# Attention, SwiGLU and eight routed experts on one core: where the overflow branch stands against the last expert's two scatters

## The chip, the core and the metric

The kernel runs on one core of a Trainium2 chip. The metric is device time in microseconds (us), the median of several runs. Inside the core five engines run their own instruction streams: TensorE (PE, with its weight loads as PEld), VectorE (DVE), ScalarE (ACT), GpSimd (POOL) and SyncE (SP). They meet only through semaphores. Each has a sequencer that runs waits, branches, register loads and DMA issues; in the trace those rows carry a q behind the engine's name (POOLq, SPq).

## The reference, cut to what matters

Three stages follow each other on 1536 tokens of width 512: an attention with local and global keys, a SwiGLU layer after an RMS norm, and a mixture of eight experts of which each token takes one. Only the last is touched:

```
logits = x @ w_gate
expert_idx = np.argmax(logits, axis=1)
...
for e in range(E):
    mask = expert_idx == e
    xe = x[mask]
    h = np.maximum(xe @ w1[e], 0.0)
    ye = h @ w2[e]
    out[mask] = gate_w[mask, None] * ye
```

The expert's width is 1024. Every row of `out` is written by exactly one expert.

## The kernel before, in words

**Two program paths.** Two input numbers, n_global and n_local, decide at run time whether a fast attention may be used. The whole of the rest, `body(is_fast)`, is built twice, and a branch of all five engines chooses (line 1339, `tc.If(fast == 1)` with `cmp.Else()`). The first copy, the fast one, runs here; the second copy's instructions lie behind it in each engine's program and are jumped over at the end.

**The experts.** Each expert has 256 slots (CAP), kept as two lists of 128 token numbers and gate weights. For each expert the kernel gathers its tokens' rows from DRAM, multiplies them with w1 (line 1044), takes the positive part on ACT and DVE (lines 1052 and 1053), multiplies with w2 (line 1022) and writes the result back. `expert_pair` does this for a whole expert, and ends in `second_layer`, which for each half of 128 tokens runs 24 matmuls into one PSUM bank `py`, scales the bank by the gate weight on ACT into a tile `yo` (line 1028), and has POOL issue an indirect DMA, the scatter, which writes the 128 rows of `yo` to the places in `out` that the token list names (line 1029):

```
1028  nc.scalar.activation(out=yo, in_=py, func=ACTF.Copy, scale=gwl[j])
1029  nc.gpsimd.indirect_dma_start(
1030      out=out, out_offset=bass.IndirectOffsetOnAxis(ap=idxl[j], axis=0),
1031      in_=yo, in_offset=None, bounds_check=NT - 1, oob_is_err=False,
```

Expert 0 goes another way in its first 128 tokens (`expert_tile`), experts 1 to 7 go through `expert_pair`. All weights of the last expert are loaded and converted long before its matmuls end.

**Tokens over capacity.** After the last expert comes `overflow` (line 1096). It counts the tokens of each expert with one small matmul, makes `need`, a row of flags, on DVE, and then every engine loads the first flag into a register (line 1111) and branches on it (line 1112, `tc.If(any_ == 1)`). With these inputs no expert has more than 256 tokens, so the branch's body is not run. The part that stands for the body not run (called the untaken side here) is not empty: on every engine it waits until the engine's own work is done and steps its semaphores by what the body would have added. For POOL this is a row of waits for the eight semaphores of its indirect DMAs, the last two scatters' among them, and then an instruction INC_SWDGE_SEM that adds to the eight. Then a branch leads to the end of the program (line 1380).

**The end.** At line 1380 SP waits for every semaphore of the program (12 rows of waits), all engines drain, POOL waits for the other four, clears the semaphores and releases them.

**What sets the order.** The order on each engine is made by a scheduler, which keeps to the program's order of the stages; the counting and the flags were already put early (near 460 us). PE, DVE, ACT and SP reach the branch as their own last instruction allows; POOL reaches it when it has issued the last scatter.

Of the kernel before, what the change touches and what calls it, by code (L numbers as in the profile page):

```python
# [8 lines left out]
F32 = mybir.dt.float32  # L9
F32R = mybir.dt.float32r  # L10
BF16 = mybir.dt.bfloat16
U32 = mybir.dt.uint32
I32 = mybir.dt.int32
ACTF = mybir.ActivationFunctionType
ALU = mybir.AluOpType
# [4 lines left out]
P = 128  # L20
B, H, S, D = 2, 8, 768, 64
NT, DM, DFF = B * S, H * D, 1536
NE, DF2 = 8, 1024
KD = DM // P
NP = H // 2
TT = NT // P
# [13 lines left out]
CAP = 256  # L40
FULL = NT
# [4 lines left out]
def kernel(  # L46
# [16 lines left out]
    nc = tc.nc  # L63
# [103 lines left out]
    rp = ctx.enter_context(tc.tile_pool(name="rp", bufs=1))  # L167
# [116 lines left out]
    for x in (tab0, tabL, tabG):  # L284
        half = const.tile([P, x.shape[1]], F32, name="half" + str(len(tabs)))
        nc.scalar.activation(out=half, in_=x, func=ACTF.Copy, scale=0.5)
        tabs.append((x, half))

    warm(WARM0)
    fast = nc.values_load(flag, min_val=0, max_val=1)  # L290

    def body(is_fast):
# [17 lines left out]
        def ps_mm(name):  # L310
            tag = banks["mm"][banks["n"] % len(banks["mm"])]
            banks["n"] += 1
            return ps(tag, {"mm": NMM, "s": NS, "pt": NPT}[tag], name)
# [698 lines left out]

        last_mm = {}

        def second_layer(hid, w2t, idxl, gwl, between):

            for j in range(len(idxl)):
                py = ps_mm("py")
                n = 0
                for m in range(DF2 // P):  # L1020
                    for a, c in ((0, 0), (0, 1), (1, 0)):
                        last_mm["py"] = nc.tensor.matmul(  # L1022
                            out=py, lhsT=hid(m, a, j), rhs=w2t[m // 2][:, c, (m % 2) * DM:(m % 2 + 1) * DM],
                            start=(n == 0), stop=(n == 23),
                        )
                        n += 1
                yo = rp.tile([P, DM], F32, tag="cv", bufs=2, name="yo")
                nc.scalar.activation(out=yo, in_=py, func=ACTF.Copy, scale=gwl[j])  # L1028
                nc.gpsimd.indirect_dma_start(  # L1029
                    out=out, out_offset=bass.IndirectOffsetOnAxis(ap=idxl[j], axis=0),  # L1030
                    in_=yo, in_offset=None, bounds_check=NT - 1, oob_is_err=False,
                )
                between()

        def expert_pair(w1t, w2t, idxl, gwl, xs, between):

            xsh, xsl = xs
            ht = []
            for m in range(DF2 // P):
                ph = ps_mm("ph")  # L1040
                n = 0
                for kk in range(KD):
                    for a, x in ((0, xsh), (0, xsl), (1, xsh)):
                        nc.tensor.matmul(  # L1044
                            out=ph[:, 0:CAP], lhsT=w1t[kk][:, a, m * P:(m + 1) * P], rhs=x[:, kk, :],
                            start=(n == 0), stop=(n == 3 * KD - 1),
                        )
                        n += 1
                if m % 2 == 0:
                    ht.append(hid_tile("eh"))  # L1050
                hi, lo = (ht[-1][:, a, (m % 2) * CAP:(m % 2 + 1) * CAP] for a in range(2))
                nc.scalar.activation(out=hi, in_=ph[:, 0:CAP], func=ACTF.Relu)  # L1052
                nc.vector.scalar_tensor_tensor(  # L1053
                    out=lo, in0=ph[:, 0:CAP], scalar=0.0, in1=hi.bitcast(F32), op0=ALU.max, op1=ALU.subtract
                )
                between()
            second_layer(
                lambda m, a, j: ht[m // 2][:, a, (m % 2) * CAP + j * P:(m % 2) * CAP + (j + 1) * P],
                w2t, idxl, gwl, between,
            )  # L1060

        def expert_tile(w1t, w2t, idx, gw, xs, between, high_first=False):
# [30 lines left out]
            )  # L1093


        def overflow(eb):
            XC = (FULL - CAP) // CAP
            cn = ps("x", 1, "cn")
            nc.tensor.matmul(out=cn[:, 0:NE], lhsT=ones, rhs=ohsum, start=True, stop=True)
            cnt = eb.tile([P, NE], F32, name="cnt")  # L1100
# [5 lines left out]
            for c in range(XC):  # L1106
                nc.vector.tensor_scalar(
                    out=need[:, 1:].rearrange("p (e c) -> p c e", c=XC)[:, c, :], in0=cnt[0:1, :],
                    scalar1=float(CAP * (c + 1)), scalar2=None, op0=ALU.is_gt,
                )  # L1110
            any_ = nc.values_load(need[:, 0:1], min_val=0, max_val=1)  # L1111
            with tc.If(any_ == 1):
                SLOTS = FULL - CAP
# [184 lines left out]
        def idx(e):  # L1298
            return [tks[:, 2 * e + j - 1:2 * e + j] for j in range(2)]

        def gw(e):
            return [wts[:, 2 * e + j - 1:2 * e + j] for j in range(2)]
# [4 lines left out]
        for e in range(NE):  # L1307
# [17 lines left out]
            if e == 0:  # L1325
                x = expert_tile(w1t.pop(0), w2t.pop(0), tks[:, 0:1], wts[:, 0:1], xs.pop(0), between)
                for _ in range(KD):
                    next(x)
                turn_rows(xg.pop(1), x=x1, js=(1,), after=last_mm["ph"])
                xs[1] = x1[:, 0], x1[:, 1]  # L1330
                drain(x)
            else:
                expert_pair(w1t.pop(e), w2t.pop(e), idx(e), gw(e), xs.pop(e), between)
        overflow(rp)
        ea_cm.__exit__(None, None, None)
        bctx2.close()

# [2 lines left out]
        body(True)  # L1340
    with cmp.Else():
        body(False)


def bits(x):
# [39 lines left out]
```

## Time and profile before

| what | value |
|---|---|
| median of 3 runs | 655.94 us (652.44 to 659.27) |
| the profiled execution | 662.28 us |
| its span (first to last instruction) | 660.2 us |
| time around the span | 2.08 us |
| PE busy | 637.3 us (97% of the span) |
| DVE, ACT, POOL busy | 445.2, 318.2, 187.3 us |
| mean granted clock of PE | 0.957 |

The profile is that of one execution, with times from the span's start. "Idle before" is what an engine waited ahead of an instruction, and the arrow names what ended that wait. Busy time leaves out sequencer rows (waits, branches, register loads), though they take time on their engine; they are found by the line that they belong to.

### The profile page before, as it was taken

How to read it: one execution, taken by the hardware profiler on the slowest of the kernel's cores; microseconds unless marked ns; L12 is line 12 of the kernel's file. 1: busy time of each engine (PE TensorE's matmuls, PEld its weight loads, DVE VectorE, ACT ScalarE, POOL GpSimd, SP SyncE). 2: the span in 40 equal slices, each digit the busy share in tenths (PEclk: the TensorE clock that was granted, in tenths of full speed). 3: DMA queues.
4: the chain of work that ended last, by engine and by line, in shares of the span. 5: the costliest groups of instructions: out<-in, count | busy, mean ns of one | idle time of the engine just before them, and what ended most of it. 6: DMA issues, size and time to landing. Idle time of an engine off the chain costs nothing. (4 is left out here: it accounts for less than half of the span.)

```text
span 660.2 us, 11655 instructions
## 1 busy us (share of the span) xinstructions
PE 637.3 (97%) x4280; PEld 570.1 (86%) x4281; DVE 445.2 (67%) x1090; ACT 318.2 (48%) x624; POOL 187.3 (28%) x259
## 2 busy tenths in 40 slices
PE   8999989999999999999999999999999999999991
PEld 3577989999999999999999999997888898899891
DVE  3845699987389998676349998953667565664410
ACT  2745678788465553334622211343656464554410
POOL 4432265354121232121122523471611121011000
PEclk9955789999999999999999999999999999999997
DMA  7644456742015443221311020342877668454001
GB/s 226 159 144 111 116 166 179 201 122 60 7 36 157 131 157 97 65 97 65 128 64 38 28 65 33 99 144 96 288 265 257 209 205 266 156 190 141 17 12 31
DMA packets 56567, 82.98 MB, mean 126 GB/s; under 512 B 7983, under 2 KB 38703, under 8 KB 56496
## 3 DMA queue, kind: packets, MB, share of 16 engines
q1 hardware_dynamic: 53552, 74.75, 37.0%
q0 software_dynamic: 2944, 7.35, 3.3%
q8 instruction: 37, 0.61, 0.4%
q14 instruction: 34, 0.28, 0.1%
HBM read 75.75 MB, written 7.39 MB: 126 GB/s over the span
## 5 line engine op out<-in xcount | busy, mean ns | idle before, releaser
L774 PE MATMUL pg<-xn,gv 128*128 128x256 f32 x1728 | 225.1, 283 | 0.2 <-DVE hf L787 0.2
L774 PEld LDWEIGHTS pg<-xn,gv 128*128 128x128 f32 x1728 | 217.1, 190 | 6.3 <-DVE hf L787 0.7
L811 PE MATMUL po<-ow,hid 128*128 128x512 f32 x432 | 113.8, 396 | 1.1 <-POOL hid L792 1.0
L792 POOL TENSOR_TENSOR hid<-hf,hid 128x256 fp32r<-128x256 f32 x72 | 63.5, 884 | 163.3 <-ACT hid L791 163.2
L1022 PE MATMUL py<-ew,eh 128*128 128x512 f32 x384 | 91.2, 395 | 1.2 <-ACT eh L1088 0.8
L811 PEld LDWEIGHTS po<-ow,hid 128*128 128x128 f32 x432 | 75.9, 188 | 13.7 <-POOL hid L792 1.5
L1022 PEld LDWEIGHTS py<-ew,eh 128*128 128x128 f32 x384 | 71.3, 188 | 18.0 <-ACT eh L1088 1.0
L1044 PE MATMUL ph<-xs,ew 128*128 128x256 f32 x672 | 83.1, 283 | 0.0
L1044 PEld LDWEIGHTS ph<-xs,ew 128*128 128x128 f32 x672 | 81.6, 191 | 0.7
L791 ACT ACTIVATE hid<-hf 128x256 fp32r<-128x256 f32 x72 | 29.8, 416 | 80.7 <-DVE hf L787 79.2
L1029 POOL DMA_INDIRECT out_dram<-yo,tk x16 | 16.5, 1034 | 138.5 <-ACT yo L1028 106.9
L843 DVE CUSTOM_DVE_ANT_0 jk<-duo,rgb 128x512 bf16<-128x512 f32 x64 | 54.3, 848 | 0.5
L962 DVE TENSOR_TENSOR ew<-rawe,ew 128x1024 fp32r<-128x1024 f32 (+1 forms) x36 | 40.8, 1134 | 13.0 <-ACT ew L958 10.9
L567 ACT ACTIVATE pr<-pr,mx 128x256 f32<-128x256 f32 (+1 forms) x96 | 42.3, 483 | 14.3 <-DVE mx L563 14.3
L1053 DVE SCALAR_TENSOR_TENSOR eh<-ph,eh 128x256 fp32r<-128x256 f32 x56 | 23.2, 422 | 37.9 <-ACT eh L1052 36.7
L782 ACT ACTIVATE th<-pg 128x256 f32<-128x256 f32 x72 | 27.1, 379 | 41.0 <-PE pg L774 40.6
L962 DVE TENSOR_TENSOR ew<-duo,ew 128x1024 fp32r<-128x1024 f32 x28 | 34.1, 1224 | 18.0 <-ACT ew L958 17.0
L958 ACT ACTIVATE ew<-rawe 128x1024 fp32r<-128x1024 f32 x36 | 38.1, 1059 | 10.7 <-PE pg L774 4.7
L1052 ACT ACTIVATE eh<-ph 128x256 fp32r<-128x256 f32 x56 | 21.1, 384 | 39.3 <-PE ph L1044 38.3
L783 DVE SCALAR_TENSOR_TENSOR th<-th,pg 128x256 f32<-128x256 f32 x72 | 29.7, 414 | 14.5 <-ACT th L782 13.5
L958 ACT ACTIVATE ew<-duo 128x1024 fp32r<-128x1024 f32 x28 | 29.4, 1059 | 19.4 <-PE py L1022 19.4
L820 DVE TENSOR_TENSOR duo<-duo,po 128x512 f32<-128x512 f32 x36 | 23.3, 682 | 22.2 <-PE po L811 22.1
(179 smaller groups left out, 930.3 us busy)
## 6 DMA issues: line engine op xcount, KB each, us to landing
rawe<-in_moe_w_dram SPq DMA_DIRECT2D x36, 512.0 KB, 4.9
duo<-in_moe_w_dram SPq DMA_DIRECT2D x28, 512.0 KB, 5.6
raw<-in_moe_w_gate_dram SPq DMA_DIRECT2D x12, 512.0 KB, 4.1
raw<-in_moe_w_val_dram SPq DMA_DIRECT2D x12, 512.0 KB, 6.0
raw<-in_moe_w_out_dram SPq DMA_DIRECT2D x12, 512.0 KB, 3.5
kn<-in_k_dram SPq DMA_DIRECT2D x28, 192.0 KB, 3.2
qn<-in_q_dram SPq DMA_DIRECT2D x36, 128.0 KB, 3.2
vn<-in_v_dram SPq DMA_DIRECT2D x16, 192.0 KB, 2.6
```

The costliest lines, as they stand in the source:

```text
L567: pin["act"] = nc.scalar.activation(out=pr[:, j, 0:n], in_=pr[:, j, 0:n], func=ACTF.Exp, bias=mx[:, t, j:j + 1], scale=-1.0,)
L774: nc.tensor.matmul(out=pg[:, 0:n_], lhsT=gv[:, i, a, kk, :], rhs=x[st][:, kk, :], start=(n == 0), stop=(n == 3 * KD - 1),)
L782: pin["th"] = nc.scalar.activation(out=th, in_=pss[0][:, 0:n_], func=ACTF.Tanh, scale=0.5)
L783: nc.vector.scalar_tensor_tensor(out=th, in0=th, scalar=1.0, in1=pss[0][:, 0:n_], op0=ALU.add, op1=ALU.mult)
L791: nc.scalar.activation(out=hh[:, 0], in_=hf, func=ACTF.Copy)
L792: nc.gpsimd.tensor_tensor(out=hh[:, 1], in0=hf, in1=hh[:, 0].bitcast(F32), op=ALU.subtract)
L811: nc.tensor.matmul(out=po, lhsT=hid[mi][:, a, t * P:(t + 1) * P], rhs=ow[:, c, :], start=(mi == 0 and n == 0), stop=(mi == len(ms) - 1 and ...
L843: nc.vector.tensor_tensor_reduce(out=jk, in0=part[i0 + t], in1=rgb[e // 4][:, e % 4, :], scale=1.0, scalar=0.0, op0=ALU.mult, op1=ALU.add, ...
L958: cp = nc.scalar.activation(out=t[:, 0], in_=raw, func=ACTF.Copy)
L962: nc.vector.tensor_tensor(out=t[:, 1, 0:nd], in0=raw[:, 0:nd], in1=t[:, 0, 0:nd].bitcast(F32), op=ALU.subtract)
L1022: last_mm["py"] = nc.tensor.matmul(out=py, lhsT=hid(m, a, j), rhs=w2t[m // 2][:, c, (m % 2) * DM:(m % 2 + 1) * DM], start=(n == 0), stop=( ...
L1044: nc.tensor.matmul(out=ph[:, 0:CAP], lhsT=w1t[kk][:, a, m * P:(m + 1) * P], rhs=x[:, kk, :], start=(n == 0), stop=(n == 3 * KD - 1),)
```

## The change

1. `overflow` is cut in two. `overflow_need` (the counting and the flags) is called ahead of the last expert, `overflow` (the flag's load and the branch) after its matmuls, with its code unchanged.
2. The last expert no longer scatters in `second_layer`. Its first half is scaled by ACT as before, but into `yof[0]`, one half of the tile `duo[5]`, which lives outside both program paths. Its second half stays in a PSUM bank of another tag ("x"), which `second_layer` returns.
3. Behind the overflow branch, DVE scales that bank into `yof[1]` (new line 1351).
4. The last expert's token numbers are copied by DVE into `ixf`, a tile outside both paths.
5. The two scatters of the last expert are issued by POOL behind the join of the two program paths, from `yof` and `ixf`. They stand there once, for both paths.

```diff
+    yof = part[TT - 2:]
+    ixf = const.tile([P, 2], U32, name="ixf")
+    def scatter(yo, ix):
+        nc.gpsimd.indirect_dma_start(
+            out=out, out_offset=bass.IndirectOffsetOnAxis(ap=ix, axis=0),
+            in_=yo, in_offset=None, bounds_check=NT - 1, oob_is_err=False,
+        )
...
-        def second_layer(hid, w2t, idxl, gwl, between):
+        def second_layer(hid, w2t, idxl, gwl, between, end=False):
             for j in range(len(idxl)):
-                py = ps_mm("py")
+                py = ps("x", 1, "py") if end and j else ps_mm("py")
...
-                yo = rp.tile([P, DM], F32, tag="cv", bufs=2, name="yo")
+                if end and j:
+                    return py
+                yo = yof[0] if end else rp.tile([P, DM], F32, tag="cv", bufs=2, name="yo")
                 nc.scalar.activation(out=yo, in_=py, func=ACTF.Copy, scale=gwl[j])
-                nc.gpsimd.indirect_dma_start(
-                    out=out, out_offset=bass.IndirectOffsetOnAxis(ap=idxl[j], axis=0),
-                    in_=yo, in_offset=None, bounds_check=NT - 1, oob_is_err=False,
-                )
+                if not end:
+                    scatter(yo, idxl[j])
                 between()
...
-        def overflow(eb):
-            XC = (FULL - CAP) // CAP
+        XC = (FULL - CAP) // CAP
+        def overflow_need(eb):
             cn = ps("x", 1, "cn")
...
+            return need
+        def overflow(eb, need):
             any_ = nc.values_load(need[:, 0:1], min_val=0, max_val=1)
             with tc.If(any_ == 1):
...
             else:
-                expert_pair(w1t.pop(e), w2t.pop(e), idx(e), gw(e), xs.pop(e), between)
-        overflow(rp)
+                if e == NE - 1:
+                    need = overflow_need(rp)
+                    nc.vector.tensor_copy(ixf, tks[:, 2 * e - 1:2 * e + 1])
+                py = expert_pair(w1t.pop(e), w2t.pop(e), idx(e), gw(e), xs.pop(e), between, e == NE - 1)
+        overflow(rp, need)
+        nc.vector.tensor_scalar(out=yof[1], in0=py, scalar1=gw(NE - 1)[1], scalar2=None, op0=ALU.mult)
...
     with cmp.Else():
         body(False)
+    for j in range(2):
+        scatter(yof[j], ixf[:, j:j + 1])
```

What it moves on the engines is seen best on POOL. Before, on the fast path, POOL's last scatters stand ahead of the load of the flag (`need`) and of the branch; the brackets name the semaphores waited for, and DMASW0 to DMASW7 are those of POOL's own DMAs:

```order
L1029 DMA out_dram<-yo,tk_5872 1536x512 [waits DMASW1_49,DMASW0_49,Activation_49]
L1029 DMA out_dram<-yo,tk_5872 1536x512 [waits DMASW1_49,Activation_49]
L1029 DMA out_dram<-yo,tk_5872 1536x512 [waits DMASW2_49,Activation_49]
L1111 TENSOR_LOAD need [waits DVE_49]
L1112 COMPARE_AND_BRANCH
```

Then follow the body that isn't run and the untaken side, which ends POOL's fast path; the ISA row here is INC_SWDGE_SEM. The two scatters of the last expert have moved away from here in the changed kernel: there the row ahead of the load is the last scatter of expert 6, in the same program place.

```order
L293 DMA out_dram<-yo,tk_5873 1536x512 [waits DMASW7_49,DMASW0_49,Activation_49]
L293 DMA out_dram<-yo,tk_5873 1536x512 [waits DMASW1_49,DMASW0_49,Activation_49]
L1124 TENSOR_LOAD need [waits DVE_49]
L1125 COMPARE_AND_BRANCH
```

They now end POOL's program. The last rows of the listing are those of the second copy's untaken side (line 1125) and its branch to the join (line 1356), and then, for both copies, the scatters (line 293); the fast copy has rows like the first three of its own, and comes from them to the first line 293:

```order
L1125 ISA [waits Pool_49,Pool_sequencer_49,DMASW4_49,DMASW5_49,DMASW3_49,DMASW6_49,DMASW2_49,DMASW7_49,DMASW1_49,DMASW0_49]
L1125 UNCONDITIONAL_BRANCH
L1356 UNCONDITIONAL_BRANCH
L293 DMA out_dram<-duo_118,ixf 1536x512 [waits DMAHW2_49,DMAHW3_49,DMASW2_49,DMAHW6_49,DMASW1_49,DMAHW7_49,DMASW0_49,Activation_49]
L293 DMA out_dram<-duo_118,ixf 1536x512 [waits DMASW3_49,DMASW2_49,DVE_49]
L1399 UNCONDITIONAL_BRANCH
L1399 ISA [waits barrier_Pool_Activation_PE_DVE_SP_gather]
```

On PE the last rows of the program are now three unconditional branches, where before there was the first alone (PE's untaken side, line 1112 then):

```order
L1125 UNCONDITIONAL_BRANCH [waits PE_49,PE_sequencer_49]
L1356 UNCONDITIONAL_BRANCH
L1399 UNCONDITIONAL_BRANCH
```

On DVE the new scaling stands between its untaken side and the branch over the second copy:

```order
L1125 UNCONDITIONAL_BRANCH [waits DVE_49,DVE_sequencer_49]
L1351 TENSOR_SCALAR duo_118<-py,wt_5874 128x512 [waits DVE_49,PE_49]
L1356 UNCONDITIONAL_BRANCH
```

Rows of that kind stand in the order wherever a block of the program ends, also where the next block stands right behind it. POOL's program starts so in the kernel before: the branch at line 1380 leads to the memset that follows it.

```order
L1362 MEMSET const-float32-1.0 128x1
L1362 MEMSET const-bfloat16-1.0 128x1
L1362 MEMSET const-uint8-127 128x1
L1380 UNCONDITIONAL_BRANCH [waits barrier_Pool_Activation_PE_DVE_SP_gather]
masks.py:197 MEMSET ident 128x128
```

Nothing moves in those rows; only their line numbers change. On PE no other row moves than those above. On ACT the second scaling is gone and its load of the flag follows the first.

## Rows read from the trace of the kernel before

**Rows 1.** Stretch, us, busy (instructions) of PE, PEld, DVE, ACT, POOL; clock, DMA, GB/s.
```profile
630.00:646.00 16.00, 16.00 (x93) 13.99 (x92) 2.12 (x5) 2.41 (x6) 0.97 (x1) 1.00 0.05 19
646.00:661.00 15.00, 0.64 (x3) 0.19 (x1) 0.00 (x0) 0.69 (x1) 0.97 (x1) 0.69 0.06 15
```

**Rows 2.** Timeline 640 to 661: start, us, engine, line, operation, [idle before <-releaser].
```profile
639.75 6.89 PE L1022 MATMUL py<-ew,eh 128*128 128x512 f32 x29
...
642.36 0.97 POOL L1029 DMA_INDIRECT out_dram<-yo,tk  x1 [14.64 <-ACT yo L1028]
646.73 0.69 ACT L1028 ACTIVATE yo<-py,wt 128x512 f32<-128x512 f32 x1 [4.64 <-PEq L1112]
647.69 0.97 POOL L1029 DMA_INDIRECT out_dram<-yo,tk  x1 [4.36 <-ACTq L1112]
```

**Rows 3.** POOL, line 1112: ns min/median/max, first and last start; the long wait alone.
```profile
L1112 POOLq EVENT_SEMAPHORE  x1: 3201/3201/3201, 648.6 to 648.6; - x1
...
L1112 POOLq COMPARE_BRANCH  x2: 38/46/53, 647.8 to 653.1; - x2
L1112 POOLq INC_SWDGE_SEM  x1: 1068/1068/1068, 652.0 to 652.0; - x1
```

**Rows 4.** Line 1380, POOL and SP: same columns, POOL's long DRAIN alone and the end.
```profile
L1380 POOLq DRAIN  x1: 3752/3752/3752, 655.6 to 655.6; - x1
...
L1380 POOLq DRAIN  x2: 40/74/107, 659.6 to 659.9; - x2
...
L1380 SPq EVENT_SEMAPHORE  x12: 28/28/28, 653.0 to 653.7; - x12
L1380 SPq DRAIN  x2: 7/10/13, 653.8 to 653.9; - x2
```

**Rows 5.** Lines 1112 and 1380 on PE, ACT and DVE: the branch and the drain behind it.
```profile
L1112 PEldq COMPARE_BRANCH  x2: 3815/4168/4521, 642.7 to 647.0; - x2
...
L1380 PEldq DRAIN  x1: 72/72/72, 651.6 to 651.6; - x1
...
L1112 ACTq COMPARE_BRANCH  x2: 38/42/45, 647.1 to 647.7; - x2
...
L1380 ACTq DRAIN  x1: 67/67/67, 651.7 to 651.7; - x1
...
L1112 DVEq COMPARE_BRANCH  x2: 47/62/78, 636.4 to 637.2; - x2
...
L1380 DVEq DRAIN  x1: 66/66/66, 640.5 to 640.5; - x1
```

**Rows 6.** The chain that ended last, its two DMA pieces of the last scatters: start, us.
```profile
626.74 2.59 DMA out_dram<-yo,tk
...
642.36 4.26 DMA out_dram<-yo,tk
```

**Rows 7.** Two DVE groups by line: ns min/median/max of scaling and adding 128x512.
```profile
L820 DVE TENSOR_TENSOR duo<-duo,po x36: 673/680/690, 231.9 to 449.4; 128x512 f32<-128x512 f32 x36
...
L339 DVE TENSOR_SCALAR cv<-cv x36: 409/420/953, 18.5 to 306.9; 128x512 f32<-128x512 f32 x36
```

**Rows 8.** A DVE copy of 128x8 by line, and DVE near 480 us.
```profile
L891 DVE COPY oh<-ohsum x6: 170/171/333, 9.7 to 436.1; 128x8 bf16<-128x8 bf16 x6
...
481.04 1.28 DVE L1089 TENSOR_TENSOR eh<-trh,eh 128x512 fp32r<-128x512 f32 x2
```

**Rows 9.** The program's start, POOL: line 1362 and the first row behind it.
```profile
L1362 POOLq EVENT_SEMAPHORE  x2: 17/17/17, 0.6 to 0.7; - x2
...
L1362 POOLq DRAIN  x1: 169/169/169, 0.4 to 0.4; - x1
...
0.83 0.20 POOL masks.py:197 MEMSET ident<- 128x128 f32 x1 [0.29 <-POOLq L1362]
```

**Rows 10.** POOL's timeline near 431 us, a DMA and what follows it.
```profile
430.72 0.97 POOL L922 DMA_INDIRECT meta_d<-meta,addr  x1 [0.30 <-issue]
431.71 1.29 POOL L966 TENSOR_TENSOR ew<-rawe,ew 128x512 fp32r<-128x512 f32 x1
```

More of the change, by code (lines that the diff above doesn't have):

```diff
@@ L1026, in second_layer, with expert_pair @@
                         n += 1
-                yo = rp.tile([P, DM], F32, tag="cv", bufs=2, name="yo")
+                if end and j:
+                    return py
+                yo = yof[0] if end else rp.tile([P, DM], F32, tag="cv", bufs=2, name="yo")
                 nc.scalar.activation(out=yo, in_=py, func=ACTF.Copy, scale=gwl[j])
-                nc.gpsimd.indirect_dma_start(
-                    out=out, out_offset=bass.IndirectOffsetOnAxis(ap=idxl[j], axis=0),
-                    in_=yo, in_offset=None, bounds_check=NT - 1, oob_is_err=False,
-                )
+                if not end:
+                    scatter(yo, idxl[j])
                 between()
-        def expert_pair(w1t, w2t, idxl, gwl, xs, between):
+        def expert_pair(w1t, w2t, idxl, gwl, xs, between, end=False):
             xsh, xsl = xs
@@ L1056, in expert_pair @@
                 between()
-            second_layer(
+            return second_layer(
                 lambda m, a, j: ht[m // 2][:, a, (m % 2) * CAP + j * P:(m % 2) * CAP + (j + 1) * P],
-                w2t, idxl, gwl, between,
+                w2t, idxl, gwl, between, end,
             )
```

## Prediction, made before the changed kernel was run

> **What bounds the kernel now.** First the busy time by stretch: up to the last matmul the kernel is bound by PE, which is busy in all 16 of the 16 us from 630 to 646 [rows 1]. The change touches nothing that PE does there. In the last 15 us, though, PE is busy for 0.64 us, ACT 0.69, POOL 0.97: none of the engines computes, and something else fills 13 us [rows 1]. So the question is what fills them.
>
> The timeline gives the beginning of that tail. The last 24 matmuls end at 639.75 + 6.89 = 646.64. ACT scales from 646.73 to 647.42, and POOL's last scatter starts at 647.69 [rows 2]. From there on only sequencer rows are left, so the next view is the source line of the branch, 1112, and that of the end, 1380. On POOL a wait of 3.20 us starts at 648.6 and ends at 651.8: the untaken side waits for the scatter that was just issued, which so took 651.8 - 647.7 = 4.1 us to land. INC_SWDGE_SEM follows at 652.0 with 1.07 us, the second branch at 653.1 [rows 3]. The first row behind it, a DRAIN, starts at 655.6: the branch over the second copy cost 2.5 us. The DRAIN lasts 3.75 us, to 659.4, and only then POOL collects the others and the program ends at 660.2 [rows 4].
>
> SP is the other one that ends late: its 12 waits start at 653.0, when INC_SWDGE_SEM has done its additions, and it arrives at 653.9 [rows 4]. PE is there at 651.6, ACT at 651.7, DVE at 640.5 [rows 5]. Hence between 653.9 and 659.4 everyone waits for POOL alone, for a branch and a drain that need no data.
>
> **What the change does to each step.**
>
> *POOL's untaken side, INC_SWDGE_SEM and the branch over the second copy go ahead of the last two scatters.* There they wait for expert 6's last scatter, issued at 626.74 and landed 2.59 us later, at 629.3 [rows 6]. With 1.07 for INC_SWDGE_SEM and 2.5 for the branch POOL is through at 633.0. Its next work, the first of the moved scatters, starts at 642.36 after an idle time of 14.64 us [rows 2]. That idle time hides all of it, with 9 us to spare; were the 3.75 us of the DRAIN really a late effect of INC_SWDGE_SEM, they would end at 636.7 and be hidden too. Without the cover the price would be what it is now, 3.6 us. Gone from the path: 1.07 + 2.5 us, and the wait rows around them (0.2).
>
> *The second scaling moves from ACT to DVE, behind DVE's branch.* DVE comes to its branch at 636.4 and would be through the untaken side at 637.2 [rows 5], 9 us before the matmuls end, so it waits for PE as ACT did. No row of before shows DVE scaling a 128x512 bank. Below it stands the scaling of a tile in SBUF (0.42 us, median), above it the sum of a bank and a tile (0.68) [rows 7]. I take 0.69, what ACT took [rows 2], since the row that reads the bank is the nearer one; both ends give 0 to 0.3 us of gain. So the last scatter starts at 647.7 as before. DVE then has its branch over the second copy left: 640.5 - 637.2 = 3.3 us [rows 5], done by 650.8, before SP. ACT's branch (651.7 - 647.7 = 4.0 us) falls to about 642, hidden.
>
> *The scatter itself is unchanged.* It lands at 651.8 if it takes the same 4.1 us. The last three landings of the trace that can be read lie between 2.59 and 4.26 us [rows 6], so it could be earlier by 1.5 or later by 0.1; I keep 4.1, the same transfer at the same moment. The Trainium skill (DMA: Bandwidth & Descriptors, section Anatomy of one DMA) gives such a DMA 2.0 us plus its bytes over 436 GB/s, by which 256 KB would land in 2.6 us, an estimate from that page; the trace's row for this very transfer says 4.1 and decides, and what a landing in 2.6 us would do stands among the rivals.
>
> *POOL's DRAIN now follows the scatter directly.* This is the unknown. Its duration is 0.17 us at the program's start, behind memsets [rows 9], 0.11 and 0.04 in the two later ones, and 3.75 in the one that counts [rows 4]. If it starts when POOL has issued the scatter (647.69 + 0.97 = 648.7), it ends between 648.8 and 652.4, in either case ahead of SP. If it first waits until the scatter has landed, it ends between 652.0 and 655.6. I take the first, as the DRAIN of before started a full 3.8 us after the landing and so does not look like a wait for it.
>
> *SP's 12 waits* now are released by the landing, 651.8, not by INC_SWDGE_SEM at 653.0. They and the drains take 653.9 - 653.0 = 0.9 us [rows 4], so SP arrives at 652.7, last of all: POOL 652.4 at most, PE 651.6, DVE 650.8.
>
> *The rest:* the copy of the token numbers is one small DVE instruction, 0.17 us like the 128x8 copy, set between the two subtractions near 481 us [rows 8], where PE may wait for it: 0 to 0.2 us. The bank of tag "x" and the tile `yof` are free long before.
>
> **Sum.** The barrier was released at 659.4 by POOL and would be at 652.7 by SP; what follows (0.8 us) is unchanged. Gain 6.7 us, of which some 3.8 are INC_SWDGE_SEM, its waits and the branch, and the rest is the drain, which now lies beside the landing, less SP's 0.9: span 660.2 to 653.5, the profiled execution 662.28 to 655.6. That execution was 6.3 us above the median of the runs; the tail holds fixed latencies, so I take the same 6.7 us from the median: 655.94 - 6.7 = 649.2 us, or 1.0%. A measurement of this kernel can tell about 1% from no change, so this sits on the very edge. Its own range is 7.0 us of gain (a shorter scaling) to 6.3 (the copy exposed, the landing at 4.26): 648.9 to 649.6, with the spread of the runs (half a per cent) 646 to 652.5.
>
> **The rivals.**
>
> *The scatter lands early,* after 2.59 us as expert 6's did [rows 6], since POOL and ACT no longer jump at the same moment. Then SP could arrive at 647.7 + 2.59 + 0.9 = 651.2, and PE at 651.6 is last. Gain 7.8 us: 648.1 us. Against it: the transfer near 642 met no such jumps and took 4.26. The rule on DMAs of the Trainium skill (DMA: Bandwidth & Descriptors, cited above) would give this case too.
>
> *The drain waits for the landing.* For it: 3.75 us is far over what a pipeline of POOL needs, and the scatter is POOL's only open business. Against it: the DRAIN of before lay long after the landing and was as long all the same. Then POOL arrives at 651.8 + 3.75 = 655.6, the gain is 3.8 us: 652.1 us.
>
> *The drain's end is tied to the scatter's issue, whatever stands between,* so that moving the branch does nothing: POOL would still be done 11.7 us after 647.69, at 659.4. For it: nothing in the trace says what the DRAIN waits for. Against it: near 431 us POOL starts a computation 0.99 us after such a DMA [rows 10], so the engine is free long before 11.7 us. The change would not do what it says: 655.9 us.
>
> *Three branches on PE instead of one, on the slower side.* In the order of the changed kernel PE's program ends in three unconditional branches, each behind the last matmul, since the untaken side waits for it. One cost 4.52 us [rows 5]. If all three are run at that price, PE arrives at 647.0 + 3 x 4.52 = 660.5 and the barrier goes 1.1 us later than now: 657.1 us. This decides from the point where the two added ones cost more than 1.1 us together (652.7 - 651.6). Against it: the second and third lead to what stands right behind them, or nearly so; at the program's start the same kind of row (line 1380, unconditional, to the block right behind it) stands in the order, and the trace has no branch there: between POOL's semaphore row at 0.7 and its first MEMSET at 0.83 is no room for one [rows 9]. Only one of the three, the one over the second copy, is a real jump. The Trainium skill (Runtime: NRT & Kernel Launch, section Instruction fetch mechanics) says that a taken branch to a place outside the fetched window waits for a DMA fetch of it; it agrees with 2.5 to 4.5 us a branch in the trace, and by it only the jump over the second copy pays.
>
> **How the numbers follow.** Forecast 0.65, early landing 0.09, drain behind the landing 0.11, nothing gained 0.07, PE's branches 0.05, anything else 0.03. In the forecast's case the gain lies on both sides of 6.6 us, which is 1%, so half of it counts as faster by over 1% (0.32), and of the early landing most (0.07); with 0.02 from the rest 0.41. Slower by over 1% would need more than any rival's price, so it takes the spread of the runs on top: 0.05. Within 1%: 0.54. The range goes from the fast end of the forecast (645) to the case without gain (656), and leaves out the slower one.
>
> **What would show it.** Right: in the changed profile POOL's INC_SWDGE_SEM stands near 630 and its branch ends before 640; the last scatter still starts about 1.1 us after the last matmul; POOL's DRAIN ends by 6 us after that matmul; SP is the last to arrive; span minus the end of the last matmul falls from 13.6 to about 6.9 us. Wrong: a DRAIN that ends more than 7 us after the last matmul (second or third case), branch rows of PE that stand in a row behind the last matmul (the slower case), or a last scatter that starts later than before because DVE or POOL comes late out of its branch.

## The result and the profile after

| | kernel before | changed kernel |
|---|---|---|
| median of 6 runs each | 656.80 us (652.44 to 659.27) | 648.64 us (645.94 to 651.17) |
| ratio | | 0.9881, 95% interval 0.9836 to 0.9926 |
| later, 29 and 12 runs | 657.17 us | 650.89 us, ratio 0.9908, 0.9883 to 0.9933 |
| profiled execution, span | 662.28, 660.2 us | 651.17, 649.4 us |
| mean granted clock in it | 0.957 | 0.971 |

The changed kernel is faster by about 1%. The later comparison is the narrower one: 657.17 x (1 - 0.9908) = 6.0 us, with an interval of 4.4 to 7.7 us. The profiled execution of the kernel before (662.28 us) and one of the 12 later runs of the changed kernel (657.85 us) are slow ones at a lower granted clock, so the ratio leaves the latter out, and the spans of the two profiles are no measure of the gain.

The last expert first: the busy time of the same two stretches as in [rows 1], some 4.7 us earlier in the program; columns as there.

```profile
626.00:642.00 16.00, 15.98 (x89) 13.52 (x87) 1.70 (x4) 2.22 (x5) 0.97 (x1) 1.00 0.06 20
642.00:650.00 8.00, 0.00 (x0) 0.00 (x0) 0.75 (x1) 0.00 (x0) 0.97 (x1) 0.78 0.09 25
```

PE is full to its last matmul as before; behind it 7.4 us are left where 13.6 were. The timeline of this end, answering to [rows 2]:

```profile
632.77 9.21 PE L1031 MATMUL py<-ew,eh 128*128 128x512 f32 x39
...
637.64 0.97 POOL L293 DMA_INDIRECT out_dram<-duo,ixf  x1 [14.62 <-ACTq L1125]
642.02 0.75 DVE L1351 TENSOR_SCALAR duo<-py,wt 128x512 f32<-128x512 f32 x1 [10.29 <-PE py L1031]
643.05 0.97 POOL L293 DMA_INDIRECT out_dram<-duo,ixf  x1 [4.43 <-DVE duo L1351]
```

The last matmul ends at 632.77 + 9.21 = 641.98. All times below that are called "behind M" count from that point of the run they belong to. The last scatter starts at 643.05, 1.07 behind M; before it was 1.05. What POOL does around its untaken side, answering to [rows 3] (line 1125 is the flag's branch, 1356 the join, 1399 the end):

```profile
L1125 POOLq INC_SWDGE_SEM  x1: 1028/1028/1028, 625.0 to 625.0; - x1
...
L1356 POOLq COMPARE_BRANCH  x1: 38/38/38, 626.0 to 626.0; - x1
```

INC_SWDGE_SEM and the jump over the second copy now start 17 and 16 us ahead of M, in POOL's idle time of 14.62 us. The end on POOL and SP, answering to [rows 4]:

```profile
L1399 POOLq DRAIN  x1: 5737/5737/5737, 642.8 to 642.8; - x1
...
L1399 SPq EVENT_SEMAPHORE  x12: 28/28/20757, 626.0 to 647.4; - x12
L1399 SPq DRAIN  x2: 7/10/13, 647.4 to 647.5; - x2
```

SP's wait from 626.0 (625.96 without rounding) ends 20.76 us later, at 646.7: that is the landing of the last scatter, 4.7 behind M. SP is at the barrier at 647.5. POOL's DRAIN has its row from 642.8, ahead of the scatter's issue (643.05 to 644.02), so such a row's length says little and its end is what counts; it ends at 648.5, 6.57 behind M and 1.0 behind SP. So POOL is still the last to arrive. PE and DVE, answering to [rows 5]:

```profile
L1356 PEldq COMPARE_BRANCH  x1: 4581/4581/4581, 642.4 to 642.4; - x1
...
L1399 PEldq DRAIN  x2: 8/44/79, 647.1 to 648.9; - x2
...
L1399 DVEq DRAIN  x2: 10/38/65, 645.4 to 648.8; - x2
```

PE has one far branch of 4.58 us behind M and arrives at 647.1; DVE jumps from 642.0 and arrives at 645.4.

**Where the difference of the two profiles comes from.** The spans differ by 660.2 - 649.4 = 10.8 us. The end accounts for 13.58 - 7.42 = 6.2. The other 4.66 are there because the last matmul ends at 641.98 and not at 646.64. Two rows say where most of these arose, the stretch from 32 to 80 us in both kernels, before first, after second. A third shows the same stretch in run 11 below, whose kernel is the changed one up to M:

```profile
32.00:80.00 48.00, 47.56 (x234) 39.37 (x232) 25.61 (x84) 25.69 (x53) 14.07 (x25) 0.55 0.43 119
```

```profile
32.00:80.00 48.00, 46.42 (x282) 39.44 (x283) 31.14 (x103) 31.26 (x67) 15.56 (x28) 0.72 0.49 135
```

```profile
32.00:80.00 48.00, 44.29 (x324) 38.48 (x323) 36.19 (x113) 35.53 (x77) 18.02 (x33) 0.89 0.56 155
```

PE is busy nearly all of the time in the first two, but does 234 instructions in the one and 282 in the other: the granted clock is 0.55 and 0.72, a mix of the two levels, 1.2 and 2.4 GHz. In run 11 it is 0.89. The change touches nothing there. Whether the 4.66 us are nevertheless owed to the change is a question for the runs.

### The profile page after: what moved, and what is told of

Its sections match the earlier page's. It is cut to its first block, busy times and chain, and to the rows that moved or that the text cites. A ratio compares the mean times of both kernels' runs of the same rounds, so it can differ in the third digit from the quotient of the medians.

```text
span 649.4 us, 11658 instructions
## 1 busy us (share of the span) xinstructions
PE 631.9 (97%) x4280; PEld 566.7 (87%) x4281; DVE 446.1 (69%) x1092; ACT 317.5 (49%) x623; POOL 187.6 (29%) x259
## 5 line engine op out<-in xcount | busy, mean ns | idle before, releaser
L820 PEld LDWEIGHTS po<-ow,hid 128*128 128x128 f32 x432 | 75.9, 188 | 13.6 <-POOL hid L801 1.1
L293 POOL DMA_INDIRECT out_dram<-yo,tk x14 | 14.6, 1040 | 120.4 <-ACT yo L1039 92.8
```

The lines of the kernel that those rows point to most:

```text
L820: nc.tensor.matmul(out=po, lhsT=hid[mi][:, a, t * P:(t + 1) * P], rhs=ow[:, c, :], start=(mi == 0 and n == 0), stop=(mi == len(ms) - 1 and ...
```

## The experiments

Each run's own last matmul is the zero point again. The theories at the start: POOL's DRAIN has a price of its own of some 3.7 us wherever it stands (own price, theory A below); it waits for the scatter, and its end counts from the landing (landing, theory B); or it is a late effect of INC_SWDGE_SEM (theory C).

**1. The scatters ahead of the join instead of behind it.**

```diff
+        for j in range(2):
+            scatter(yof[j], ixf[:, j:j + 1])
         ea_cm.__exit__(None, None, None)
...
-    for j in range(2):
-        scatter(yof[j], ixf[:, j:j + 1])
```

> Both scatters stay behind the overflow branch but go ahead of the branch over the second copy, so on POOL that branch (2.5 us) stands again between the last scatter and the DRAIN. All times from the end of the last matmul; in the changed kernel the last scatter starts at 1.1, lands at 4.7, SP arrives at 5.5, POOL's DRAIN ends at 6.6, the span at 7.4. Theory A, the DRAIN has a cost of its own of about 3.75 us from where POOL comes to it: the branch is run while the scatter is being issued, the DRAIN starts near 3.6 and ends at 7.4 or later, the span at 8.2 to 9. Theory B, the DRAIN waits for the scatter (its landing or the POOL work behind it) and ends about 1.9 us behind the landing: the branch is hidden, DRAIN ends at 6.6 and the span at 7.4, as in the changed kernel. If the place behind the join itself is what brings the time: span near 10, 2.5 us later.

Measured: 654.70 us, span end 8.58 behind M. POOL's branch and DRAIN and SP's wait in this kernel (line 1358 is its join):

```profile
L1358 POOLq COMPARE_BRANCH  x1: 38/38/38, 645.3 to 645.3; - x1
...
L1399 POOLq DRAIN  x3: 40/107/3751, 648.4 to 652.7; - x3
...
L1399 SPq EVENT_SEMAPHORE  x14: 17/28/20561, 628.5 to 652.9; - x14
```

M is 644.44. The jump takes from 645.3 to 648.4, 3.1 us, and lies beside the scatter's issue and transfer; the DRAIN's 3.75 us then follow, to 7.73, as theory A said. It is as long here, starting ahead of the landing (628.5 + 20.6 = 649.1), as in [rows 4], where it started 3.8 us after it. The place behind the join is worth 8.58 - 7.42 = 1.2 us against the first profile, and 2.0 against run 5.

**2. Ten fills of POOL between the scatter and the DRAIN.**

```diff
+    for _ in range(10):
+        nc.gpsimd.memset(yof[1], 0.0)
```

> Ten memsets of 128x512 on POOL between the last scatter and the DRAIN; they wait until that scatter has landed (4.7 us from the end of the last matmul) and overwrite the tile that it read. Theory A, the DRAIN has a cost of its own wherever it stands: it ends 3.75 us or more behind the last memset. Theory B, it waits for what the scatter leaves, which is over 1.9 us behind the landing: when the memsets take 2 us or more the DRAIN ends within 0.2 us of the last one.

Measured: 656.83 us. The fills in the timeline, and the DRAIN by its line (1401):

```profile
644.77 5.77 POOL L1363 MEMSET duo<- 128x512 f32 x10 [2.72 <-DMA out_dram<-duo,ixf]
```

```profile
L1401 POOLq DRAIN  x3: 40/113/4239, 650.0 to 654.8; - x3
```

The last fill ends at 650.54; the DRAIN's row begins in it and ends at 654.24, 3.70 behind it and 9.5 behind the landing. So here it neither runs beside other work of POOL nor counts from the landing.

**3. No last scatters** (the last expert's 256 rows are not written).

```diff
-    for j in range(2):
-        scatter(yof[j], ixf[:, j:j + 1])
```

> The last expert's two scatters are left out (its 256 rows of the output are not written). POOL comes to its DRAIN right behind its branch over the second copy, 13 us ahead of the last matmul's end. Theory A, a cost of its own: the DRAIN takes 3.75 us there. Theory B, it waits for the last scatter: about 0.2 us, since expert 6's landed long before; if INC_SWDGE_SEM leaves work behind it (theory C), some 3.7 us, the DRAIN ending 6.3 us behind INC_SWDGE_SEM as in the kernel before. The span then ends with PE's branch: DRAIN of PE at 5.1 us from the last matmul's end, span at 5.9, 1.5 us ahead of the changed kernel, by all theories.

Measured: 647.09 us, span end 6.1 behind M. POOL's DRAIN now stands right behind its jump:

```profile
L1397 POOLq DRAIN  x3: 40/107/3587, 625.9 to 645.1; - x3
...
L1356 PEldq COMPARE_BRANCH  x1: 4741/4741/4741, 639.6 to 639.6; - x1
```

3.59 us at 625.9, some 4 us after the last landing (that of expert 6's last scatter), with nothing issued in between. The late effect falls with run 2, where the price is paid 26 us after INC_SWDGE_SEM. What is left of the tail here is PE's jump, 639.6 + 4.74 = 644.4: a floor that the scatters have nothing to do with.

**4. Only the very last scatter moved**; the first half's stays ahead of the flag's branch.

```diff
-                if not end:
-                    scatter(yo, idxl[j])
+                scatter(yo, idxl[j])
...
-    for j in range(2):
-        scatter(yof[j], ixf[:, j:j + 1])
+    scatter(yof[1], ixf[:, 1:2])
```

> Only the second half's scatter stands behind the join; the first half's is issued ahead of the overflow branch as in the kernel before. POOL's waits at the branch then are for that first scatter, which lands near the last matmul's end (0.0 us), and INC_SWDGE_SEM (1.05) and the branch (2.5) come behind it. My theory (what gains is that POOL is through its branch before the last half is ready): last scatter starts at 3.7 instead of 1.1, lands at 7.4, span ends near 10.0 us from the last matmul's end, against 7.4 changed and 13.6 before. Rival (only the last scatter's place counts): 7.4 as changed.

Measured: 651.66 us, span end 11.4 behind M (M 638.55). POOL's line of the flag's branch, and then its timeline:

```profile
L1124 POOLq INC_SWDGE_SEM  x1: 1048/1048/1048, 638.9 to 638.9; - x1
```

```profile
644.47 0.97 POOL L293 DMA_INDIRECT out_dram<-duo,ixf  x1 [9.28 <-issue]
```

POOL waits for the first half's scatter to land, so INC_SWDGE_SEM starts 0.35 behind M and the jump follows; the last scatter starts 5.92 behind M, 4.85 late. The expectation put it at 3.7: the jump took 3.3 us and not 2.5, and waits on both sides of it were left out. Both scatters have to be behind the join.

**5. The changed kernel again, in 12 runs.**

> The changed kernel itself, timed in five rounds. All times below are counted from the end of the last matmul. The two profiled executions differ by 10.8 us in span, of which the end of the program shows 6.16 (13.58 against 7.42). Theory tail: the rest is the spread of the granted clock in stretches that the change does not touch, so the gain over many runs is 6.2 us give or take 1, a ratio near 0.9905. Rival elsewhere: the change also gains some 4 us ahead of the last matmul, in every run; then the gain is 9 to 11 us, a ratio near 0.985. In both the end of this profile again: scatter from 1.07, landing by 4.7, POOL's DRAIN ends near 6.6, span end near 7.4.

Measured: ratio 0.9908 (0.9883 to 0.9933), so 6.0 us: the end alone, and not 9 to 11. But the end was not that of the first profile. Its last scatter in the timeline, and then the rows of the lines 1399 and 1356:

```profile
642.52 0.97 POOL L293 DMA_INDIRECT out_dram<-duo,ixf  x1 [4.43 <-DVE duo L1351]
```

```profile
L1399 POOLq DRAIN  x1: 4889/4889/4889, 642.3 to 642.3; - x1
...
L1399 SPq EVENT_SEMAPHORE  x12: 28/28/19818, 625.4 to 645.9; - x12
...
L1356 PEldq COMPARE_BRANCH  x1: 3727/3727/3727, 641.8 to 641.8; - x1
```

M is 641.46. The landing is at 645.2, 3.8 behind M instead of 4.7; PE's jump takes 3.73 us instead of 4.58; POOL's DRAIN ends at 5.72 instead of 6.57, and the span 6.57 behind M. The same program's end varies by 0.85 us between two executions.

**6. The counting alone ahead of the last expert.**

```diff
-                py = expert_pair(w1t.pop(e), w2t.pop(e), idx(e), gw(e), xs.pop(e), between, e == NE - 1)
+                py = expert_pair(w1t.pop(e), w2t.pop(e), idx(e), gw(e), xs.pop(e), between)
...
-        nc.vector.tensor_scalar(out=yof[1], in0=py, scalar1=gw(NE - 1)[1], scalar2=None, op0=ALU.mult)
...
-    for j in range(2):
-        scatter(yof[j], ixf[:, j:j + 1])
```

> Of the change only the cut of overflow in two: the counting and the flags ahead of the last expert, the scatters and the branch as in the kernel before, no copy of the token numbers. Theory tail: nothing is gained, the end is that of the kernel before (POOL's DRAIN ends near 12.7 behind the last matmul, span end near 13.6), and the time is within 2 us of the kernel before. Rival elsewhere: if the new place of the counting gains the other 4 us ahead of the last matmul, this kernel is 4 us faster than before with the same end.

Measured: ratio 1.0008 (0.9977 to 1.0039), span end 13.3 behind M, POOL's DRAIN 3.75 us as in [rows 4]:

```profile
L1396 POOLq DRAIN  x1: 3752/3752/3752, 650.7 to 650.7; - x1
```

The copy of the token numbers, meant to be left out, stayed in (a DVE row of 0.159 us at 457.1). So the earlier counting and the copy together gain and cost nothing that can be told, within some 2 us. With run 5, the 4.66 us ahead of M are the spread of the granted clock from execution to execution, not the change: in the profiles of runs 1 to 5, 7, 11 and 12, whose kernels are the changed one up to the last expert's scatters, M itself lies anywhere from 638.06 to 644.44.

**7. A later scatter in the changed kernel.**

```diff
+    for _ in range(3):
+        nc.vector.tensor_scalar(out=yof[1], in0=yof[1], scalar1=1.0, scalar2=None, op0=ALU.mult)
```

These stand between the two scatters.

> The changed kernel, with three more scalings by 1.0 of the last half on VectorE behind the join, so that the last scatter starts when the jumps of all engines over the second copy are over (about 5.5 behind the last matmul instead of 1.07). Theory contention: the jumps' fetching of code makes the landing and POOL's DRAIN longer. Then here the landing takes 2.6 us (not 3.65) and the DRAIN ends 3.7 behind the scatter's issue end (not 4.53): landing near 8.1, DRAIN near 10.2, span end near 11.0. Rival order: both are longer because the scatter stands directly ahead of the DRAIN, with or without jumps; then landing near 9.15, DRAIN near 11.0, span end near 11.9.

Measured: 655.84 us, span end 10.5 behind M (M 643.68). The scatter started at 4.8, sooner than meant, but with PE's jump just over too (644.0 + 3.92 = 647.9 in its row). The last scatter in the timeline, then line 1401, the end of this kernel, and PE's jump:

```profile
648.47 0.97 POOL L293 DMA_INDIRECT out_dram<-duo,ixf  x1 [8.16 <-DVE duo L1362]
```

```profile
L1401 POOLq DRAIN  x3: 40/113/4886, 648.2 to 653.7; - x3
L1401 SPq EVENT_SEMAPHORE  x14: 17/28/23201, 627.9 to 654.1; - x14
...
L1356 PEldq COMPARE_BRANCH  x1: 3918/3918/3918, 644.0 to 644.0; - x1
```

Landing at 627.9 + 23.2 = 651.1, 2.6 after the start, and the DRAIN 3.68 behind the issue's end, as contention said. But run 5 has these numbers too, with both jumps beside the scatter, so this does not settle it.

**8. The two program paths in the other order**, so that the jump comes at the start.

```diff
-    with tc.If(fast == 1) as cmp:
-        body(True)
-    with cmp.Else():
-        body(False)
+    with tc.If(fast == 0) as cmp:
+        body(False)
+    with cmp.Else():
+        body(True)
```

> The changed kernel with the two program paths in the other order: the slow copy first, the fast one behind it, so that all engines jump at the start (8 to 10 us) and none at the end. Theory contention: without jumps at the end the landing takes 2.6 us and the DRAIN 3.7: SP arrives near 4.5 behind the last matmul, POOL's DRAIN ends near 5.8 and is last, span end 6.6 (0.8 sooner than the changed kernel). The start costs 0 to 4.6 us: PE's jump took 4.58, and between 8.3 and 9.7 PE only runs its warm-up, but SP issues the loads, whose transfers fill the queues from 11 to 18 us, and its jump holds these up; I expect 3 us more at the start, so 2 us slower than the changed kernel. Rival order: the end as in the changed kernel, 7.4, and 3 us slower.

Measured: 653.92 us, the median of 10 runs, ratio to the kernel before 0.9981 (0.9948 to 1.0014). That is slower than the changed kernel by 4.8 us by the ratios (0.9981 - 0.9908 of 657.17) and by 3.0 by the medians (653.92 - 650.89). The end is as contention said (M 644.29): DRAIN ends at 5.73, SP arrives at 4.5, span end 6.63. It is also the end of run 5, which had the jumps.

```profile
L1399 POOLq DRAIN  x3: 40/113/4876, 645.1 to 650.6; - x3
```

So all of the loss lies at the start. PE's jump of this kernel, and its timeline behind it:

```profile
L1356 PEldq COMPARE_BRANCH  x1: 3837/3837/3837, 8.3 to 8.3; - x1
```

```profile
14.51 0.80 PE L554 MATMUL sp<-duo 64*128 64x128 f32 x4
...
18.22 0.41 PE L587 MATMUL pp<-ident,pr 128*128 128x128 f32 x1
```

The same two places of PE's timeline in run 5:

```profile
9.83 0.49 PE L554 MATMUL sp<-duo 64*128 64x128 f32 x4
...
11.86 0.33 PE L587 MATMUL pp<-ident,pr 128*128 128x128 f32 x1
```

The first scores come 4.7 us later and the next step 6.4 later: PE stands still for its jump, and behind it the granted clock of the stretch from 8 to 16 us is 0.73, a mix of the two levels, where it was 1.00, 2.4 GHz (the same four matmuls take 0.80 us for 0.49). The two stretches, run 8 first, then run 5:

```profile
8.00:16.00 8.00, 4.04 (x13) 1.44 (x12) 2.14 (x12) 2.53 (x6) 2.98 (x10) 0.73 0.64 196
```

```profile
8.00:16.00 8.00, 7.58 (x43) 3.51 (x42) 2.73 (x18) 3.73 (x9) 2.67 (x9) 1.00 0.94 297
```

By M the two profiles are only 2.8 us apart (644.29 and 641.46). The jump is dearer at the start than at the end.

**9 and 10. One more DRAIN of POOL**, to learn whether the price is paid again.

```diff
+    nc.gpsimd.drain()
     for j in range(2):
         scatter(yof[j], ixf[:, j:j + 1])
```

Run 10 has the same line, and fills of the two tiles in place of the scatters (the last expert's 256 rows are not written).

> The changed kernel with one more DRAIN on POOL, ahead of its last two scatters, where POOL is idle for some 9 us. Theory each: a DRAIN costs 3.6 to 3.7 us behind any work of POOL. Then the added one takes 3.6 us in the idle time (about -13 to -9.5 from the end of the last matmul), and the last one ends 3.7 behind the scatter's issue end as before: 5.7, span end 6.6. Rival once: the cost is paid by the first DRAIN alone (its code has to be fetched once, or what is left of the DMAs of the whole program has to be gathered). Then the last DRAIN takes 0.2 us or less behind the issue end (2.3), SP at 4.5 is last, span end near 5.4: 1.2 us sooner than the changed kernel.

> As the run before, but the last two scatters are left out (the last expert's 256 rows are not written) and POOL fills the two tiles with zeros instead, so that between the two DRAINs POOL has two fills and no DMA. Theory each: the last DRAIN ends 3.6 to 3.7 behind the last fill. Rival once: 0.2 us or less. Third, DMA: a DRAIN is long only where POOL has issued DMAs since the one ahead of it; then 0.2 us or less here, and 3.7 in the run before.

Both missed their aim: nothing ties a DRAIN to other work, and the scheduler put it at the program's start.

```profile
L1360 POOLq DRAIN  x1: 1342/1342/1342, 1.3 to 1.3; - x1
```

It ended at 2.63, 0.06 behind the work of POOL that stood ahead of it (an IOTA, to 2.57), so it paid nothing there:

```profile
2.38 0.19 POOL L270 IOTA gi<- 128x32 int32 x1
```

The last DRAIN was long in both, run 9 (M 642.51, 651.63 us) first, then run 10 (M 644.41, 651.86 us):

```profile
L1400 POOLq DRAIN  x3: 40/113/5663, 643.3 to 649.6; - x3
```

```profile
L1400 POOLq DRAIN  x3: 40/113/4076, 645.2 to 649.9; - x3
```

It ended 4.46 us behind the issue's end, and 3.54 behind the fill. A DRAIN at 1.3 us, ahead of all of POOL's DMAs, takes nothing off the last.

**11 and 12. The same, held in its place** between the last two scatters; in run 12 a fill stands for the last scatter (128 rows of the last expert are not written).

```diff
-    for j in range(2):
-        scatter(yof[j], ixf[:, j:j + 1])
+    first = scatter(yof[0], ixf[:, 0:1])
+    with tc.issue_after(first.ins):
+        mid = nc.gpsimd.drain()
+    with tc.issue_after(mid.ins):
+        scatter(yof[1], ixf[:, 1:2])
```

> The changed kernel with one more DRAIN on POOL, held in its place between the last two scatters (in the run e9 the added one went to the program's start, and so said nothing). POOL issues the first scatter by -3.4 from the end of the last matmul, and the last one at 1.07. Theory each: a DRAIN takes 3.6 to 4.5 us behind any work of POOL: the added one from -3.4 to between 0.2 and 1.1, the last one again 3.7 to 4.5 behind the scatter's issue end, so until 5.7 to 6.6; span end 6.6 to 7.4. Rival once: only the first DRAIN pays; the last one takes 0.2 us or less, SP at 4.5 to 5.4 is last, span end 5.4 to 6.3.

> As the run before, but behind the added DRAIN POOL fills the last tile with zeros in place of the last scatter (128 rows of the last expert are not written), so that between the two DRAINs POOL issues no DMA. Theory each: the last DRAIN ends 3.5 to 4.5 behind the fill (ends near 1.4), so at 4.9 to 5.9. Third, DMA: a DRAIN is long only where POOL has issued DMAs since the DRAIN ahead of it; then it takes 0.2 us or less behind the fill, by 1.6, and PE at 4.1 to 5.2 is last. Rival once: the same as DMA here, and it is told from it by the run before.

Run 11 (M 638.06) took 647.05 us, run 12 (M 644.07) 652.05 us. The two scatters of run 11 in the timeline, and then both DRAINs and SP's wait by their lines (1402 is the end of this kernel):

```profile
633.72 0.97 POOL L293 DMA_INDIRECT out_dram<-duo,ixf  x1 [14.61 <-ACTq L1125]
...
641.03 0.97 POOL L293 DMA_INDIRECT out_dram<-duo,ixf  x1 [6.33 <-issue]
```

```profile
L1362 POOLq DRAIN  x1: 6652/6652/6652, 633.5 to 633.5; - x1
...
L1402 POOLq DRAIN  x1: 2982/2982/2982, 640.8 to 640.8; - x1
...
L1402 SPq EVENT_SEMAPHORE  x14: 17/28/21629, 622.1 to 645.3; - x14
```

The fill of run 12 in the timeline, and its last DRAIN by line:

```profile
646.20 0.52 POOL L1364 MEMSET duo<- 128x512 f32 x1 [5.50 <-issue]
```

```profile
L1402 POOLq DRAIN  x1: 597/597/597, 646.2 to 646.2; - x1
```

In run 12 the last DRAIN ends at 646.8, 0.07 behind the fill that ends at 646.72: no price. In run 11 it ends at 640.8 + 2.98 = 643.8, 0.1 behind the landing (622.1 + 21.63 = 643.7) and 1.8 behind the issue's end. So "each" falls with run 12. "Once" in the reading that the code has to be fetched once falls with run 9, where a DRAIN at 1.3 us came first and the last was long all the same. "DMA" as put expected 3.7 us in run 11, and one DMA costs no more than its landing. What fits all the runs is the other reading of "once": the 3.7 us go with what POOL has done since its last DRAIN, and besides DRAIN waits for the last landing. The likely part of it is the DMAs, without the added DRAIN all 44 indirect ones of the program (16 + 12 + 14 + 2 by the groups of POOL's DMAs), but this is argued and not shown: the DRAIN that paid was in every run also the first behind INC_SWDGE_SEM, and the first after some 600 us of other work of POOL, so that run 9 does not rule out a second fetch of its code. No run parts the three, and none shows whether the price grows with the number of DMAs. The added DRAIN itself ended at 2.1 behind M, 1.8 behind its scatter's landing, and held the last scatter up to 2.97, so run 11's end is 7.3 and nothing is gained.

## Why the prediction was right, and the step that was mis-sized

Forecast were 649.2 us and a gain of 6.7; measured are 648.64 us in the first six runs, a gain of 6.0 (4.4 to 7.7) in the longer comparison, and at the end of the program 6.2 in one profile and 7.0 in the other (13.58 - 6.57). Behind M 6.9 us were forecast, 7.42 and 6.57 measured. The 1% that a measurement can just tell was to lie on the very edge, and it does.

*POOL's untaken side, INC_SWDGE_SEM and the branch are hidden:* right. The forecast had POOL through at 633.0, 13.6 ahead of M; the branch starts at 626.0, and the next row of POOL stands 13.4 ahead of M (13.5 in run 5). Run 4 shows the cover gone: the last scatter 4.85 us later.

*The second scaling on DVE:* 0.75 us against 0.69, above the bound of 0.68 from the sum of a bank and a tile. The scatter starts 1.07 behind M for 1.05.

*The landing:* 4.1 kept, 3.7 and 2.7 measured (646.7 - 643.05 and 645.2 - 642.52). The rule of the Trainium skill (DMA: Bandwidth & Descriptors, section Anatomy of one DMA), 2.6 us as an estimate, agrees with runs 4, 5, 7, 8 and 11 (2.6 to 2.7) and not with the first profile.

*POOL's DRAIN* is the term that was mis-sized, and with it "SP arrives last". The text took it to end 0.17 to 3.75 us behind the issue, by 652.4, ahead of SP in either case. It ended 4.53 behind the issue in the first profile and 3.68 in run 5, each time last, 1.0 and 1.1 us behind SP. So two of the signs named for being right did not come: SP was not the last to arrive, and in the first profile the DRAIN did not end by 6 us. Wherever it was POOL's first behind the DMAs of the program, it ended 3.5 to 3.75 us behind POOL's last work (in run 1 that is the jump), or 1.8 behind the landing where that was later:

| run | issue ends | landing | DRAIN ends | behind issue | behind landing |
|---|---|---|---|---|---|
| first profile | 2.0 | 4.7 | 6.6 | 4.5 | 1.8 |
| 4 | 6.9 | 8.5 | 10.6 | 3.7 | 2.1 |
| 5 | 2.0 | 3.8 | 5.7 | 3.7 | 1.9 |
| 7 | 5.8 | 7.4 | 9.5 | 3.7 | 2.1 |
| 8 | 2.0 | 3.7 | 5.7 | 3.7 | 2.1 |
| 9 | 2.0 | 4.7 | 6.5 | 4.5 | 1.8 |
| 11, added one | -3.4 | 0.3 | 2.1 | 5.4 | 1.8 |

That fits the 0.8 us between the two profiles of the same kernel: the landing was 1.0 later. It is read from the rows of these runs; none was made to move the landing alone. What DRAIN does in that time no row shows. The two errors, a landing that came sooner and a DRAIN that ended later, cancel in part; that the sum came out nearer than its terms is luck.

*The rivals.* Early landing: the landing did come after 2.7 us in run 5, but POOL, not PE, was last. The argument against it, that the transfer near 642 met no such jumps and took 4.26, overlooked PE: a branch row of 3.82 us from 642.7 in [rows 5] lies beside that transfer. Drain behind the landing: not at the price given, landing + 3.75, which would be 8.5 behind M; but DRAIN does wait for the landing, as run 11 shows. Nothing gained: refuted by run 5. Three branches on PE: PE has one row of 4.58 us at line 1356 and none at 1399. The Trainium skill (Runtime: NRT & Kernel Launch, section Instruction fetch mechanics) says that a taken branch to a place outside the fetched window waits for a fetch of it; the trace agrees, with 4.58 us for the far one and no row for those to the next block.

*The copy of the token numbers* is one DVE row of 0.159 us, and by run 6, which has it too, it costs nothing that can be told in the time:

```profile
L1348 DVE COPY ixf<-tk x1: 159/159/159, 457.6 to 457.6; 128x2 uint32<-128x2 uint32 x1
```

**What stays open.** Why the landing took 2.6 to 2.7 us in runs 4, 5, 7, 8 and 11 and 3.6 to 3.7 in the first profile and in runs 1, 2 and 9. Where no jump lay beside it (4, 7, 8) or PE's alone (11), it was short. Where PE's and DVE's lay beside it, it was long in four profiles and short in run 5; beside PE's and ACT's, in the kernel before and in run 6, it took 4.1 and 3.8. So jumps go with a long landing but do not settle it. The flag's branch on PE points the same way; its row lies beside the first of the two scatters. The first profile, then run 5:

```profile
L1125 PEldq COMPARE_BRANCH  x1: 3995/3995/3995, 638.1 to 638.1; - x1
```

```profile
L1125 PEldq COMPARE_BRANCH  x1: 1652/1652/1652, 637.6 to 637.6; - x1
```

In the ten profiles where that row is 3.4 to 4.2 us long, the first scatter landed 3.9 to 4.7 us after its start (read from POOL's waits for it). In runs 5 and 7, where it is 1.7 and 1.2, the scatter landed after 3.2. No run was made to set this apart.

It also stays open which of POOL's doings since its last DRAIN the 3.7 us belong to. And a DRAIN ahead of both last scatters, in POOL's idle time, was not tried: run 9 meant to. By run 11 the last DRAIN would then end close behind the landing, SP would be last, about 1.0 us sooner; that is an estimate.

## What to carry to other kernels

At the end of a program, look for sequencer rows behind the last matmul that need no data of it (branches over code not run, semaphore additions, waits for landings), and put them on their engine ahead of the last work, where it waits anyway: here 6 us of 657. Move all that the untaken side waits for: one of two scatters left ahead of the branch gave back 4 of the 6. And when two profiles of a pair differ by more than the stage that was changed, look at the granted clock of the other stages, and let many runs say how much is the change.

## What had not been expected of the hardware

- POOL's DRAIN costs 3.5 to 3.75 us where it is POOL's first behind the DMAs of a whole program, 0.1 us behind the landing where one DMA has been issued since the last DRAIN, and 0.07 behind a fill where none has.
- A jump over the second copy costs each engine its own time: 3.7 to 4.7 us on PE, 2.8 to 4.0 on DVE, 2.5 to 3.3 on POOL. At the start of the program it cost 3.0 us of the total by the medians and 4.8 by the ratios, more than at the end.
- One and the same program's jump on PE took 4.58 and 3.73 us, and its last scatter 3.7 and 2.7 us to land, in two executions.
- From 32 to 80 us PE, busy almost throughout, was granted 0.72 of its clock in one execution and 0.89 in another, by two kernels that do not differ up to there (the changed one and run 11's), and M lay 3.9 us apart (641.98 and 638.06).
